# A fused block-sorted attention and PReLU feed-forward kernel: the order of every engine's list read from a fixed table instead of found by a random search

## The chip, the cores and the metric

The kernel runs on one core of a Trainium2 chip. The metric is the device time of one execution in microseconds (us). Five engines work side by side, each through a list of its own in strict order: TensorE (PE, matrix products), VectorE (DVE), ScalarE (ACT), GpSimd (POOL) and SyncE (SP). SP does nothing here but issue DMAs; POOL issues DMAs as well and does copies and memsets between them. A wait at the head of a list holds up everything behind it in that list.

## The reference, cut to what matters

```python
# B, H, S, D = 4, 8, 768, 64; 8 blocks of 96 rows
P = sort_net                      # five rounds: softmax over the rows, then division by the column sums
k_sorted = einsum('bhij,bhjcd->bhicd', P, k_blocks)
v_sorted = einsum('bhij,bhjcd->bhicd', P, v_blocks)
scores = scale * (q_block @ k_sorted_block.T)
attn = exp(scores - max); attn /= attn.sum(-1)
x = (attn @ v_sorted_block)       # -> [3072 tokens, 512]
h = x @ w_in                      # 512 -> 2048
g = max(h, 0) + alpha * min(h, 0)
out = g @ w_out                   # 2048 -> 512
```

## The kernel before, in words

The batch index b runs from 0 to 3. A *group* g = 8 b + i is one block of 96 tokens over all eight heads, so there are 32 groups. For each group the attention makes scores (`s1`, matmul L801 for b = 0 and L798 after that), a row maximum on DVE (`nm` or `nf`, L807), exponentials on ACT, the product with the sorted values (`o`, L854), a reciprocal and a multiplication on DVE (L862, L865). For b = 0 the scores are made again transposed (`s2`, L822 and L813), so the exponentials land as the product needs them. For b > 0 ACT writes `Esb` (eight instructions, L834) and an SP DMA transposes it to `ET` (L839). The result reaches `xT`, token-last, through four PE transposes (L880) and a copy for b < 2, through an SP DMA (L873) after that.

Before a batch can be worked on, its keys and values are mixed with the sorting matrix: `conv_k` (POOL, L701) and `conv_v` (POOL, or ACT or DVE for half of b = 1, L457) spread the loaded rows into `KSz` and `VDz`, then `prep_k` (L714) and `prep_v` (L755) multiply and a copy (L457, ACT or DVE) writes `KT` and `VS`. The queries of b = 0 are turned on PE (`prep_q`); those of b > 0 are loaded by eight DMAs into `QN` (L486) and turned by six SP DMAs into `QTz` (`turn_q`, L494), where turn t holds rows 128 t to 128 t + 127. Group 8 reads turn 0, group 9 turns 0 and 1, group 10 turns 1 and 2.

The feed-forward part is cut into chunks of tokens: groups 0-1, 2-3, then four groups at a time. `ffn1` (L904, four matmuls of 192 or 384 columns) makes one of 16 slices of h for a chunk; ACT makes relu(-h) (L914) and DVE joins the two (L917) into `hT`. `ffn2` (L943) makes a tile of 128 tokens in four parts of four matmuls with 512 columns; a copy (L457) and an SP DMA (L957) store it. The last tile is made in two halves of 256 columns.

All of this is entered by `G.add` as 1226 *operations*, numbered from 0 in the order of the calls, each with its engine (or a choice of ACT and DVE), what it reads and writes, a modelled duration and a priority. `schedule` is a list scheduler: it simulates the engines and always starts, on the engine that can go first, the ready operation of the smallest priority. `search` calls it 2000 times with the priorities shifted at random (500 times for the stage up to the first `xT`, 1500 times for the rest), each promising order being replayed twice with durations up to 8% longer, and keeps the best. `fetched` adds to the PE's simulated time the loading of its program, 256 instructions at a time, `FETCH` = 6200 ns apart at least. After that, `fill` and `idle` put matmuls without use (`warm`, L1070) into gaps that the simulation sees on PE, and `emit` writes each engine's list with the waits that the order needs. Nothing of the simulation runs on the chip: it only fixes the order, the choice of ACT or DVE, and where the warm matmuls stand.

Of the kernel before, what the change touches and what calls it, by code (L numbers as in the profile page):

```python
# [2 lines left out]

# [22 lines left out]
NE = 3  # L26
VSL = 4
EPS = 1e-9
SEARCH = 1500
FIRST = 500  # L30
FETCH = 6200.0
BURST = 140

XLAT = {"pe": 215, "act": 36, "dve": 36, "pool": 80, "sync": 80}
ENGS = ("pool", "sync", "pe", "act", "dve")

# [37 lines left out]
class _Graph:  # L76
# [51 lines left out]
    def fetched(self, op, at, d, f):  # L128

        if f["fills"] and at > 5000:  # L130
            f["n"] += 2 * int(max(at - f["end"], 0) * 0.9 / 215)
        f["fills"] = f["fills"] and op.fills
        n, last = 2 * op.mm, f["n"] + 2 * op.mm
        while f["mark"] < last:
            x = at + d * max(f["mark"] - f["n"], 0) / n
            late = max(f["usable"] - x, 0.0)
            at, x = at + late, x + late
            f["usable"] = x + FETCH
            f["mark"] += 256
        f["n"], f["end"] = last, at + d  # L140
        return at + d

    def ready_at(self, op, e):
        t = 0.0
        for d in op.deps:
            x = self.ops[d]
            if x.eng != e or x.dma:
                lat = XLAT[x.eng]
            else:
# [3 lines left out]
            t = max(t, x.end + lat)  # L153
        return t

    def schedule(self):
        ops = self.ops
        for op in ops:
            op.users, op.eng = [], op.engs
        for op in ops:  # L160
            op.left = len(op.deps)
            for d in op.deps:
                ops[d].users.append(op.idx)
        ready = {e: [] for e in ENGS}

        def release(op):
            op.ready = {}
            for e in op.engs:
                op.ready[e] = self.ready_at(op, e)
                ready[e].append(op)  # L170
# [4 lines left out]
        order = {e: [] for e in ENGS}  # L175
        for op in ops:
            if not op.left:
                release(op)
        done = 0
        while done < len(ops):  # L180
            best = None
            for e in ENGS:
                if not ready[e]:
                    continue
                first = max(free[e], min(o.ready[e] for o in ready[e]))
                op = min((o for o in ready[e] if o.ready[e] <= first + 60), key=lambda o: (o.prio, o.idx))
                first = max(first, op.ready[e])
                if best is None or first < best[0]:
                    best = (first, e, op)
            at, e, op = best  # L190
            for x in op.engs:
                ready[x].remove(op)
            op.eng, op.start = e, at
            free[e], op.end = self.span(op, e, at, free, loads)
            op.pos = len(order[e])
            order[e].append(op)
            done += 1
            for u in op.users:
                ops[u].left -= 1
                if not ops[u].left:  # L200
                    release(ops[u])
        self.order = order
        return max(op.end for op in ops)

    def replay(self, seed):

        rng = random.Random(seed)
        was = [(op.start, op.end) for op in self.ops]
        free = dict.fromkeys(ENGS, 0.0)
        free["pool"] = 400.0  # L210
        loads = [0.0, 0.0, {"n": 2, "mark": 193, "usable": 0.0, "end": 0.0, "fills": True}]
        for op in sorted(self.ops, key=lambda o: (o.start, o.idx)):
            at = max(free[op.eng], self.ready_at(op, op.eng))
            free[op.eng], op.end = self.span(op, op.eng, at, free, loads, 0.08 * rng.random())
        last = max(op.end for op in self.ops)
        self.ends = [op.end for op in self.ops]
        for op, (a, b) in zip(self.ops, was):
            op.start, op.end = a, b
        return last

    def search(self, n, first):

        rng = random.Random(7)
        rank = [op.prio for op in self.ops]
        best = None
        for x in range(FIRST + n):
            if x == FIRST:
                best = None
            lo, hi, part = (-47.5, 3.0, 0.2) if x < FIRST else (0.0, 99.0, 0.1)
            amp = rng.choice((0.1, 0.3, 1.0))  # L230
            for op, p in zip(self.ops, rank):
                op.prio = p + (rng.uniform(-amp, amp) if x % FIRST and lo < p < hi and rng.random() < part else 0.0)
            cost = self.schedule()
            if x < FIRST:
                cost = sum(op.end for op in first)
            if x < FIRST or best is None or cost < best + 1500:
                for seed in (1, 2):
                    late = self.replay(seed)
                    cost += sum(self.ends[op.idx] for op in first) if x < FIRST else late
                cost /= 3  # L240
                if best is None or cost < best:
                    best, rank = cost, [op.prio for op in self.ops]
                    if __import__("os").environ.get("SCHED"):
                        print("search", x, round(cost))
        for op, p in zip(self.ops, rank):
            op.prio = p
        return self.schedule()

    def fill(self, make, unit, first, spans):

# [118 lines left out]
def bass_sinkhorn_attn__then__act_prelu_kernel(  # L369
# [23 lines left out]
    PE, ACT, DVE, POOL, SYNC = ("pe",), ("act",), ("dve",), ("pool",), ("sync",)  # L393
# [3 lines left out]
    bz = sb("bz", [128, 32], BF16)  # L397
# [61 lines left out]
    def t_either(n, mode=1):  # L459
# [4 lines left out]
          w=["P"], prio=-100, dma=(dma_sem("sn"), 0))  # L464
# [266 lines left out]
    first_y, first_x = [], []  # L731
# [233 lines left out]
    def burst(e):  # L965
# [26 lines left out]
    for p in range(2):  # L992
# [14 lines left out]
    for ga, gb in chunks:  # L1007
        w = gb - ga
# [3 lines left out]
        last = gb * BLK // 128  # L1012
# [7 lines left out]
    for g in range(NG + 12):  # L1020
        while fp < len(ffn_plan) and ffn_plan[fp][0] < g:
            pr, kind, a = ffn_plan[fp]
# [7 lines left out]
        b, i = g // NB, g % NB  # L1030
# [84 lines left out]
```

## Time and profile before

| | |
|---|---|
| median of 3 runs | 249.02 us (248.68 to 249.65) |
| the profiled execution, its own time | 249.8 us |
| its span, first to last instruction | 248.1 us |
| PE busy | 234.3 us, 94% |
| DVE, ACT, POOL busy | 171.5, 155.1, 101.1 us (69%, 63%, 41%) |
| warm matmuls (L1070) | 44 |
| mean granted TensorE clock | 0.979 of full speed |

The profile gives, for one execution, the busy time of each engine; the *chain of waits*, followed back from the last instruction, whose pieces stand with their start, length and line; and groups of equal instructions with their count and mean duration. A matmul's duration there is longer than its share of PE's time, since matmuls overlap: four matmuls of 512 columns last 379 ns each, yet take 0.86 us together on the chain. So PE's work is counted from the chain's pieces, not from busy time. A DMA's row gives the time from its issue to its landing.

### The profile page before, as it was taken

What the parts mean: (1) busy time and instruction counts of PE and PEld (TensorE: products, weight loads), DVE (VectorE), ACT (ScalarE), POOL (GpSimd) and SP (SyncE); (2) the same over time, 40 slices, a digit from 0 to 9 for tenths busy, and PEclk for the clock granted to TensorE, in tenths of its full rate; (3) what the DMA queues carried; (4) which work ended last, traced back from release to release, by engine and by line L of the source; (5) the groups of instructions that cost most, each with busy time, mean ns of one, the idle gap of its engine ahead of it and who ended that gap; (6) DMA issues with size and microseconds to landing.
All of it is one profiled execution on the core that took longest, in us unless ns stands there. A gap on an engine that the chain in (4) does not pass through costs nothing.

```text
span 248.1 us, 6269 instructions
## 1 busy us (share of the span) xinstructions
PE 234.3 (94%) x2538; PEld 145.0 (58%) x2538; DVE 171.5 (69%) x347; ACT 155.1 (63%) x423; POOL 101.1 (41%) x146
## 2 busy tenths in 40 slices
PE   6876899999999979999999999999999999999995
PEld 3445567668655636666565666655556555555544
DVE  6764667669787878786679878676869476655510
ACT  5567335596868876786648567965685576455511
POOL 8988902275899967798554103100000000000000
PEclk9999579999999999999999999999999999999999
DMA  6999999999999899989985665532364232301112
GB/s 104 208 211 210 173 215 205 172 196 124 193 85 185 156 170 143 140 121 132 145 135 132 93 159 108 132 94 53 87 122 107 49 103 45 95 11 73 44 45 86
DMA packets 71982, 31.37 MB, mean 126 GB/s; under 512 B 64512, under 2 KB 67344, under 8 KB 71952
## 3 DMA queue, kind: packets, MB, share of 16 engines
q0 software_dynamic: 23408, 13.63, 41.1%
q1 hardware_dynamic: 48544, 17.33, 36.5%
q8 instruction: 20, 0.33, 0.6%
q14 instruction: 10, 0.08, 0.2%
HBM read 27.28 MB, written 6.29 MB: 135 GB/s over the span
## 4 chain that ended last, share of the span: by engine, by line
PE 81%; DMA 8%; ACT 4%; DVE 3%; POOL 2%; issue 2%; POOLq 0%
PE psH L904 31%; PE psYP L943 28%; DMA VST<-in_v_dram 5%; PE psS L943 3%; PE psO L854 3%; PE psS L798 3%; DMA ET<-Esb 3%; PE psYP L755 2%; POOL VDz L457 2%; PE psYP L714 1%; PE psS L813 1%; PE psYP L1070 1%; ACT VDz L457 1%; DVE hT L917 1%; PE psS L822 1%
## 5 line engine op out<-in xcount | busy, mean ns | idle before, releaser
L917 DVE SCALAR_TENSOR_TENSOR hT<-t,omaT,psH 128x384 bf16<-128x384 f32 (+1 forms) x139 | 77.4, 571 | 31.7 <-ACT t L914 29.8
L904 PE MATMUL psH<-xT,w_in_bf 128*128 128x384 bf16 (+1 forms) x556 | 97.8, 312 | 0.6 <-DVE hT L917 0.3
L914 ACT ACTIVATE t<-psH 128x384 f32<-128x384 f32 (+1 forms) x139 | 62.8, 465 | 48.4 <-PE psH L904 44.3
L943 PE MATMUL psYP<-w_out_bf,hT 128*128 128x512 bf16 x336 | 84.7, 379 | 0.3 <-DVE hT L917 0.3
L904 PEld LDWEIGHTS psH<-xT,w_in_bf 128*128 128x128 bf16 x556 | 49.9, 98 | 33.0 <-DVE hT L917 5.9
L834 ACT ACTIVATE Esb<-psS,nf 96x96 bf16<-96x96 f32 x192 | 46.3, 345 | 1.2 <-DVE nf L807 0.9
L943 PEld LDWEIGHTS psYP<-w_out_bf,hT 128*128 128x128 bf16 x336 | 30.4, 98 | 27.4 <-DVE hT L917 0.4
L457 POOL COPY VDz<-VST 64x384 bf16<-64x384 bf16 x40 | 34.0, 851 | 13.6 <-PE psYP L755 11.6
L701 POOL COPY KSz<-KS 64x512 bf16<-64x512 bf16 x36 | 22.2, 618 | 33.0 <-PE psYP L714 21.0
L807 DVE TENSOR_REDUCE nf<-psS 96x8 f32<-96x768 f32 x24 | 22.7, 946 | 0.9 <-PE psS L798 0.9
L865 DVE TENSOR_TENSOR xq<-psO,rec 96x512 bf16<-96x512 f32 x31 | 21.2, 685 | 1.0
L486 POOL DMA_DIRECT2D QN<-in_q_dram x24 | 19.8, 848 | 2.5 <-DMA QTz<-QN 1.2
L854 PEld LDWEIGHTS psO<-VS,ET 112*128 112x128 bf16 x248 | 11.5, 100 | 6.9 <-ACT Esb L834 2.0
L854 PE MATMUL psO<-VS,ET 112*128 112x65 bf16 x248 | 13.1, 196 | 1.8 <-DMA ET<-Esb 1.5
L798 PEld LDWEIGHTS psS<-KT,QTz 128*96 128x96 bf16 x192 | 11.7, 125 | 2.7
L798 PE MATMUL psS<-KT,QTz 128*96 128x96 bf16 x192 | 12.6, 208 | 0.0
L862 DVE RECIPROCAL rec<-psO 96x8 f32<-96x8 f32 x31 | 6.1, 198 | 9.2 <-PE psO L854 9.1
L1070 PE MATMUL psYP<-identb 128*128 128x512 bf16 x34 | 11.3, 468 | 1.0 <-ACT identb L457 1.0
L457 ACT ACTIVATE VS<-psYP 112x512 bf16<-112x512 f32 x13 | 8.9, 687 | 5.0 <-PE psYP L755 3.2
L457 DVE CAST VS<-psYP 112x512 bf16<-112x512 f32 x13 | 9.0, 690 | 3.7 <-PE psYP L755 3.7
L457 ACT ACTIVATE outstg<-psYP 128x512 f32<-128x512 f32 x11 | 6.6, 598 | 7.7 <-PE psYP L943 7.7
L755 PE MATMUL psYP<-BDV,VDz 128*128 128x64 bf16 x192 | 9.5, 193 | 0.5 <-POOL VDz L457 0.5
(139 smaller groups left out, 212.6 us busy)
## 6 DMA issues: line engine op xcount, KB each, us to landing
out_dram<-outstg SPq DMA_DIRECT2D x23, 256.0 KB, 2.3
KS<-in_k_dram POOLq DMA_DIRECT2D x3, 768.0 KB, 31.5
QN<-in_q_dram POOLq DMA_DIRECT2D x24, 96.0 KB, 5.5
w_in_bf<-in_moe_w_in_dram POOLq DMA_DIRECT2D x4, 512.0 KB, 17.3
w_out_bf<-in_moe_w_out_dram POOLq DMA_DIRECT2D x2, 1024.0 KB, 28.6
VST<-in_v_dram POOLq DMA_DIRECT2D x4, 384.0 KB, 31.8
hT<-in_q_dram POOLq DMA_DIRECT2D x1, 768.0 KB, 7.0
VST<-in_v_dram POOLq DMA_DIRECT2D x1, 768.0 KB, 13.4
```

What stands on the lines that cost most here:

```text
L457: return e.activation(o, i, ACTF.Copy) if e is nc.scalar else e.tensor_copy(o, i)
L486: G.add(POOL, lambda e, h=h: e.dma_start(AP(QN, h * 128 + (h // 4) * 64, [[6144, 128], [1024, 6], [1, 64]]), AP(q.tensor, b * HB + h * S * ...
L701: G.add(POOL, lambda e, hp=hp: e.tensor_copy(AP(KSz, hp * 64 * 3072 + u % 3 * 1024 + hp * 64, [[3072, 64], [128, 8], [1, 64]]), AP(KS[n], ...
L798: inst = e.matmul(o, AP(QTz[n], hp * 3072 + h4 * 768 + i * 96, [[6144, 128], [1, 96]]), AP(KT[n], (h4 * 8 + i) * bk, [[ld, 128], [64, 2], ...
L807: G.add(DVE, lambda e: e.tensor_reduce(AP(nx, 0, [[8, 96], [4, 2], [1, 4]]), AP(psX, 0, [[1024, 96], [512, 2], [96, 4], [1, 96]]), AxisLis ...
L834: inst = e.activation(AP(Esb[me], p * 128, [[1024, 96], [64, 2], [1, 48]]), AP(psX, (p // 4) * 512 + (p % 4) * 96, [[1024, 96], [48, 2], [ ...
L854: inst = e.matmul(AP(psZ, hp * 512 + h4 * 68, [[1024, 128], [1, 65]]), AP(ET[me] if far else ET[m], pos(h4, hp) * 96, [[800, nk], [1, 128] ...
L865: G.add(DVE, lambda e: e.tensor_tensor(out=AP(xq[me], 0, [[512, 96], [256, 2], [64, 4], [1, 64]]), in0=AP(psZ, 0, [[1024, 96], [512, 2], [ ...
L904: inst = e.matmul(AP(pt, poff, [[1024, 128], [1, n]]), AP(w_in_bf, kt * DFF + ft * 128, [[KT_TILES * DFF, 128], [1, 128]]), AP(xT, kt * XR ...
L914: G.add(ACT, lambda e: e.activation(AP(t1[tb], 0, [[384, 128], [1, n]]), AP(pt, poff, [[1024, 128], [1, n]]), ACTF.Relu, scale=-1.0), t_ac ...
L917: G.add(DVE, lambda e: e.scalar_tensor_tensor(out=AP(hT, ft * RING + tok % RING, [[FT_TILES * RING, 128], [1, n]]), in0=AP(t1[tb], 0, [[38 ...
L943: inst = e.matmul(AP(bank[0], bank[1], [[1024, 128], [1, n]]), AP(hT, ft * RING + tok % RING, [[FT_TILES * RING, 128], [1, 128]]), AP(w_ou ...
```

## The change

The search and its two helpers (`schedule`, `replay`, `search`) are taken out. A table `SEQ` holds all 1226 operation numbers in one sequence; `arrange` goes through it, puts each operation at the end of its engine's list, and works out the simulated start and end that `fill`, `idle` and `emit` need. A letter behind a number chooses the engine where there is a choice (`d` for DVE, `a` for ACT, none for the first of the two, ACT). Two constants of the simulation change: the distance of program loads becomes 3500, 6150, 7700 or 5200 ns by the time of the load, and the opening burst of 140 tiny matmuls is counted at 9.4 ns each instead of 8.5. The operations themselves, what they compute, their tiles and buffers and the waits' rules stay.

```diff
-import random
-SEARCH = 1500
-FIRST = 500
-FETCH = 6200.0
+SEQ = """
+0 2 10 3 4 11 7 8 1 30 28 9 14 42 43 44 29 45 5 46 47 48 6 49 50 51 147 52 53 54 12 55 56 57 27 58 148 59 60
+61 133 62 63 64 131 65 66 67 132 68 83 69 91 70 84 21 71 89 130 81 72 40 73 87 74 82 75 76 88 77 78 92 79 85
+80 39 93 90 100 94d 95 102 96d 104 103a 16 97 37 86 101d 26 98 107a 108 110d 109d 99a 32 116 106d 111 118
+105a 18 114 38 138 158 117a 115d 149 15 113a 120 150 122 112a 31 347d 151 20 121d 24 23 159 134 312d 13 123d
...
+""".split()
-            f["usable"] = x + FETCH
+            f["usable"] = x + (3500.0 if x < 3000 else 6150.0 if x < 12500 else 7700.0 if x < 30000 else 5200.0)
-    def schedule(self):
...
-    def replay(self, seed):
...
-    def search(self, n, first):
...
+    def arrange(self, table):
+        assert len(table) == len(self.ops)
+        letters = {"p": "pool", "a": "act", "d": "dve"}
         free = dict.fromkeys(ENGS, 0.0)
         free["pool"] = 400.0
         loads = [0.0, 0.0, {"n": 2, "mark": 193, "usable": 0.0, "end": 0.0, "fills": True}]
+        self.order = {e: [] for e in ENGS}
+        done = set()
+        for x in table:
+            op = self.ops[int(x.rstrip("pad"))]
+            e = letters.get(x[-1], op.engs[0])
+            assert e in op.engs and op.deps <= done
+            done.add(op.idx)
+            at = max(free[e], self.ready_at(op, e))
+            op.eng, op.start, op.pos = e, at, len(self.order[e])
             free[e], op.end = self.span(op, e, at, free, loads)
+            self.order[e].append(op)
+        return max(op.end for op in self.ops)
-    G.add(PE, burst, 200 + 8.5 * BURST, r=["bz"], w=["psSw"], prio=-120)
+    G.add(PE, burst, 200 + 9.4 * BURST, r=["bz"], w=["psSw"], prio=-120)
-    total = G.search(SEARCH, first_x)
+    total = G.arrange(SEQ)
```

To read the table one needs a few numbers: 4, 5 and 6 are the loads of q, k and v for b = 0; 147 and 148 the two halves of v for b = 1, 138 its k, 139 to 146 its q; 130 to 133 are `w_in`, 134 and 135 `w_out`; 401 and 402 are v and 403 k for b = 2; 177 to 182 are turns 0 to 5 of the queries of b = 1; 312 and 347 are `conv_v` of b = 1 for two of its eight units; 418 and 434 are the scores of groups 8 and 9. The order of the lists before is the one that the search ends in and that the trace shows. The lists then differ so:

| list | before | with the table |
|---|---|---|
| POOL, loads | q, k, v (b=0), w_in ×4, w_out ×2, k, v, v (b=1), q ×8 (b=1), v, v, k (b=2) | q, k, v (b=0), **v, v (b=1)**, w_in ×4, k (b=1), w_out, q ×2, w_out, **v (b=2)**, q ×6 (b=1), k, v (b=2) |
| SP, turns of b = 1 | 1, 0, 2, 3, 4, 5 | 0, 4, 3, 2, 5, 1 |
| SP, groups 8 to 16 | `ET` of a group, then a turn of b = 2 and the stores, in turns | `ET` of groups 8 to 13 and three stores, then turns of b = 2 one by one between further `ET` |
| POOL, groups 8 on | the eight loads of q (b=2) in one block, then `conv_v` (b=2) | `conv_v` (b=2) and `conv_k` first, loads of q between them |
| `conv_v` of b = 1 on ACT or DVE | 5 on ACT, 3 on DVE | 2 on ACT, 6 on DVE, two of these among the first 54 operations of DVE |
| PE, work in front of the scores of groups 8, 9, 16, 18, 20 (counted from the first `ffn1`) | 28.2, 31.8, 71.4, 83.6, 94.3 us | 27.2, 32.0, 66.1, 74.5, 82.9 us |
| last tile | left half, then right half | right half, then left half |

The last but one row counts the operations in PE's list with the durations that the chain of waits shows for them. All in all 219 of PE's 398 operations stand in another place relative to the rest, and 52 copies change between ACT and DVE.

More of the change, by code (lines that the diff above doesn't have):

```diff
@@ new lines @@
+620 703 751 665a 503 667 621 704 658 646 668 691 659 669 747 705 604d 692 660 629 670 630 631 719a 706 738
+673 739 671 693 674 533 672 740 632 685 633d 675 680 749 681 688 750d 777 686 741 767 689 687 753 846 690
+754a 697 776 768 700 698 778 852 699 701 694 769 702 780 720 682 723 653 779d 707 849 695a 770 802 708 782
+709 724 732 848 721 725 683 742 783a 722 811 729 803 726 696 650 730 813 731 727 733 847 814a 710 728 758
+853 804 743 744 734 781 735 652 759 805 837 812 760 815 755 816a 173 745 736d 764 756 817 757 771 818a 787
@@ new lines @@
+1061 1084 1028 1029 1037 1038 1048 1030 1039 1031 1040 1043 1041 985 1080 1042 1044 1045 1052 1085 1062 1053
+1055 1054 1081 1056 1063 1086 1064 1049 1057 1065 1066 1050d 1069 1067 1087 1115 1068 1070 1082a 1071 1104
+1072 1083 1105 1116 1073 1106 1074 1117 1092 1088 1075 1093 1107 1094 1118 1076 1089 1077 1098 1119a 1095
+1120 1099 1160 1100 1096 1090 1136 1097 1091 1108 1112 1109 1110 1101 1113 1111 1137 1114 1102 1103 1124
+1051 1121 1125 1161 1126 1122 1123 1130 1127 1131 1138 1132 1128 1129 1142 1133 1143 1162 1144 1134 1135
@@ L174, in schedule @@
         loads = [0.0, 0.0, {"n": 2, "mark": 193, "usable": 0.0, "end": 0.0, "fills": True}]
[L175 to L193, printed above, removed]
-            free[e], op.end = self.span(op, e, at, free, loads)
[L195 to L201, printed above, removed]
@@ L202, in schedule @@
-        self.order = order
-        return max(op.end for op in ops)
-    def replay(self, seed):
[L207 to L219, printed above, removed]
@@ L221, in search @@
-    def search(self, n, first):
[L223 to L247, printed above, removed]
```

47 lines of the change are left out of this document (34 added, 13 removed).

## The prediction

> **What bounds the kernel now.** I read the page first, then the chain of waits stretch by stretch, then PE's groups by shape, then the landings of the DMAs.
>
> ```profile
> by line: PE psH L904 41.0%; PE psYP L943 40.0%; PE psS L943 5.9%; PE psS L798 4.4%; PE psO L854 3.5%; PE psYP L714 1.8%; PE psYP L755 1.3%; PE psO L943 1.2%; PE psO L880 0.5%; DVE outstg L457 0.3%; issue 0.0%
> ...
> 229.37 0.86 PE psYP L943 x4
> 230.23 1.30 PE psH L904 x8
> ```
>
> The first row is the chain between 100 and 246 us: its PE shares add up to 99.6%, and PE's pieces stand end to end, as the two below it do. From 100 us on no order can win anything that PE does not do sooner; time won earlier, on the other hand, arrives at the end in full. So the question is what PE wastes before 100 us. These are its groups between the first `ffn1` (30.4 us) and 100 us:
>
> ```profile
> L943 PE MATMUL psYP<-w_out_bf,hT 128*128 128x512 bf16 x67 | 16.9, 379 | 0.3 <-DVE hT L917 0.3
> L904 PE MATMUL psH<-xT,w_in_bf 128*128 128x384 bf16 x80 | 15.6, 327 | 0.4 <-DVE hT L917 0.3
> L904 PE MATMUL psH<-xT,w_in_bf 128*128 128x192 bf16 x108 | 12.8, 255 | 0.2
> L755 PE MATMUL psYP<-BDV,VDz 128*128 128x64 bf16 x128 | 6.4, 193 | 0.5 <-POOL VDz L457 0.5
> L854 PE MATMUL psO<-VS,ET 112*128 112x65 bf16 x80 | 4.3, 197 | 1.8 <-DMA ET<-Esb 1.5 <-ACT ET L845 0.3
> L813 PE MATMUL psS<-identb,nm 96*112 96x96 bf16 x48 | 4.0, 232 | 0.0
> L880 PE MATMUL psO<-identb,xq 96*128 96x96 bf16 x40 | 3.4, 206 | 0.1
> L798 PE MATMUL psS<-KT,QTz 128*96 128x96 bf16 x48 | 3.2, 209 | 0.0
> L1070 PE MATMUL psO<-identb 128*128 128x512 bf16 x10 | 3.0, 379 | 0.0
> L904 PE MATMUL psYP<-xT,w_in_bf 128*128 128x192 bf16 x20 | 2.8, 270 | 0.2 <-ACT KT L457 0.2
> L714 PE MATMUL psYP<-BDM,KSz 128*128 128x64 bf16 x56 | 2.8, 194 | 0.0
> L822 PE MATMUL psS<-QTz,KT 64*112 64x96 bf16 x48 | 2.6, 234 | 0.0
> L1070 PE MATMUL psYP<-identb 128*128 128x512 bf16 x7 | 2.3, 417 | 0.0
> L801 PE MATMUL psS<-KT,QTz 64*96 64x96 bf16 x40 | 1.9, 214 | 0.0
> ```
>
> Their prices when nothing holds them up are pieces of the chain; the two above give 0.215 us for a matmul of 512 columns and 0.1625 us for one of 384:
>
> ```profile
> 36.74 0.34 PE psS L822 x8
> 37.08 0.54 PE psS L813 x8
> ...
> 38.28 0.33 PE psYP L904 x4
> ...
> 38.94 0.31 PE psS L801 x8
> ...
> 94.46 0.37 PE psS L798 x8
> 94.83 0.17 PE psO L880 x4
> ...
> 96.93 0.23 PE psYP L755 x8
> ...
> 100.42 0.24 PE psO L854 x8
> ```
>
> Count by price: L943 67 × 0.215 = 14.4; L904 80 × 0.1625 = 13.0 and 128 × 0.33/4 = 10.6; L755 and L714 (the same shape) 184/8 × 0.23 = 5.3; L854 10 × 0.24 = 2.4; L813 6 × 0.54 = 3.2; L822 6 × 0.34 = 2.0; L801 5 × 0.31 = 1.6; L798 6 × 0.37 = 2.2; L880 10 × 0.17 = 1.7. Together 56.4 us of work in 69.6 us: 13.2 us wasted, in which the 17 warm matmuls (17 × 0.215 = 3.7 us) ran. This is all that there is to win behind the first `ffn1`.
>
> **The change part by part, summed against the profiled execution's own 249.8 us.** That execution lies 0.8 us above the median of the runs shown, 249.02, so the sum's result is moved to the median at the end.
>
> *The start.* The loads run through POOL's queue one after the other.
>
> ```profile
> 2.86 13.41 DMA VST<-in_v_dram
> ...
> L988 POOL DMA_DIRECT2D w_in_bf<-in_moe_w_in_dram x4: 548/563/576, 4.3 to 5.9; - x4
> DMA to landing us min/median/max: 14.4/17.3/20.4
> ...
> L520 POOL DMA_DIRECT2D VST<-in_v_dram x2: 612/618/623, 8.7 to 9.2; - x2
> DMA to landing us min/median/max: 34.8/35.6/36.5
> ...
> 30.43 0.82 PE psH L904 x4
> ```
>
> The v of b = 0 lands at 16.3 us; `w_in` is complete at 5.9 + 20.4 = 26.3, 4.1 us before the first `ffn1`. The two halves of v for b = 1 land at 43.5 and 45.7, 2.2 us apart, so the pair costs 4.4 us of the queue. The table puts the pair ahead of `w_in`, which then lands at 30.7: the cover is gone, and `ffn1` cannot start before 30.7 (+0.3 us). What v of b = 1 gains: it lands at 20.7 instead of 45.7, so `conv_v` can run in the thin stretch before 30 us. But 347 and 312 stand in DVE's list ahead of most copies of `VS` for b = 0 (six of eight are DVE's now). Behind a late v there would wait the copies of `VS`, then `o` of groups 0 and 1, then everything. Between 16.3 us and 347 DVE has three conversions of v, one copy and one row maximum to do, so I have it reach 347 about when that v lands, and the first `ffn1` ready at 30 to 31 us as before. Bounds: 0, and +1.9 us, the length of the one bare stall of the chain in this stretch (next fence, "issue": PE had no work to wait for there, so I read it as a wait for its program). I take +0.3 us, hidden by the next bound.
>
> *From the first `ffn1` to the scores of group 9.* PE's list before holds 31.8 us of work there (128 small `ffn1` matmuls 10.6, eight parts of `ffn2` 6.9, twelve large `ffn1` matmuls 1.95, twelve preparations 2.8, six groups of b = 0 9.6) and takes 71.33 − 30.43 = 40.9 us: 9.1 us of the waste lie here.
>
> ```profile
> 21.76 1.91 issue
> PEclk9999579999999999999999999999999999999999
> ...
> 50.23 0.86 ACT VDz L457
> ...
> 71.33 0.47 PE psS L798 x8
> ...
> L494 SPq DMA_TRANSPOSE QTz<-QN x6: 1312/1860/5588, 51.4 to 65.1; - x6
> DMA to landing us min/median/max: 3.2/5.5/10.0
> ```
>
> Three things make it. Behind the stall the granted clock falls: a slice is a fortieth of the span, 6.2 us, so 0.5 and 0.7 in the fifth and sixth say half clock from about 25 to 34.5 us, and the 4.1 us of it behind 30.4 cost 2.0. ACT's `conv_v` copies (five in this batch at 0.86 us, one of them quoted) stand on the chain between its relu's, while PE waits for `hT`; the table leaves two on ACT. And warm matmuls fill what the old simulation saw as gaps; a new order can only lessen the need for them (in gaps they cost nothing; if all 17 stood in the way, 3.7 us). Worth up to 7 us, then, but a DMA caps it. The scores of group 9 need turns 0 and 1. Before, the last turn landed at 65.1 + 3.2 = 68.3 us. With the table turn 1 is the last of the six; the turns start when the q's have landed, which is 2.2 us later than 51.4 because half of v for b = 2 goes first; in exchange that much less load runs beside the turns, so I keep 68.3 for the last. The scores of group 9 can come forward from 71.33 to 68.3 at most: 3.0 us. PE would need 30.7 + 32.0 = 62.7 us without any waste, so it may still waste 5.6 us of the 9.1 and reach the cap. I take 2.0 us. Bounds: 3.0, and −1.9 if the stall and half clock come once more.
>
> *From the scores of group 9 to 100 us.* Here 13.2 − 9.1 = 4.1 us are wasted.
>
> ```profile
> 80.01 0.84 POOL VDz L457
> ...
> 85.99 6.39 DMA ET<-Esb
> ...
> ET<-Esb SPq DMA_TRANSPOSE x24, 3.0
> ```
>
> PE ran out of work behind two chains: POOL's copies for b = 2, the last of five in a row at 0.84 us, held back by the block of eight loads of q in front of them; and the transpose of group 10, 6.39 us from issue to landing where the median of all 24 is 3.0. It flew together with turns of b = 2 and loads. The table takes both out of the way: `conv_v` stands before the loads of q, and the `ET` of groups 8 to 13 go ahead of all turns of b = 2. What is late next: `prep_k` of b = 2 and its turns, needed only for group 16. Its scores, though, are asked for 5.3 us of PE work earlier than before. I take 2.0 us. Bounds: 3.5, and −1.5, the idle time that PE had once for an `ET` (in the row of L854 above), should it come again for a turn of b = 2.
>
> *Behind 100 us, and the end.* PE is full, and the scores stand 5 to 11 us of PE work earlier than before for groups 16 to 20, so the `ET` have more cover: nothing to win, and a list in which ACT or DVE is late is covered by what the longer lead leaves. The halves of the last tile change places and each ends with a copy and a store: 0.
>
> Sum: 249.8 − 2.0 − 2.0 = 245.8 us; at the level of the median, 245.0 us.
>
> By the Trainium skill, "TensorE: Matmul & The Clock Gate", Part 1 on the clock gate, the clock falls to half only behind a whole idle window of about 3.4 us. The trace does not agree: the clock fell behind a stall of 1.9 us. By the page a table with gaps under 3.4 us wins the 2.0 us of half clock for certain; by the row it can lose them to the next stall of 1.9 us, and the sum goes by the row.
>
> **The rivals.**
>
> *All of it comes back.* PE reaches the cap (3.0) and the stretch behind it loses almost nothing (3.5): 249.02 − 6.5 = 242.5 us. For it: five separate causes of waste are moved at once. Against it: a list in strict order meets its waits one by one, and the simulation's durations are not the chip's.
>
> *A wait takes the place of the one removed.* PE comes to the scores of group 8 and 9 earlier and stands before turn 1; the `ET` still collide, now with the loads of k and v for b = 2, which are issued later than before. The turns end 2.2 us later, at 70.5, the gain up to group 9 shrinks to 71.3 − 70.5 = 0.8 us, and behind it nothing comes back: 249.02 − 0.8 = 248.2 us. For it: the first turn starts 2.2 us later, and one that was needed first has become the last.
>
> *Slower: the start slips.* The place is DVE's list in front of the copies of `VS`, the price a later first `ffn1`. If v of b = 1 lands later than 20.7 us, or PE's program stall of 1.9 us falls behind it, the first `ffn1` moves to 32.6 us, half clock reaches 2 to 4 us further into it (1 to 2 us more lost, say 1.5), and only half of the 2.0 behind group 9 comes back: 249.02 + 1.9 + 1.5 − 1.0 = 251.4 us. It decides from the point where the start's slip exceeds what is won up to group 9, 2.0 us. For it: the cover of `w_in` falls from 4.1 to 0 us. Against it: v of b = 0 landed exactly when the queue's order says.
>
> **How the numbers follow.** The forecast 0.45, all of it 0.20, the wait in place 0.13, slower 0.22. The forecast's own range is 243.5 to 246.8 us, 0.75 more or 0.9 less in each of the two stretches. For eight in ten I reach down to 241.5, 1 us under the best case, and up to 250.8, into the slower case; the worst bounds of both stretches together (249.02 + 1.9 + 1.5 = 252.4) stay outside. Faster by over 0.5% (what a measurement of this kernel can tell from no change, 1.25 us) means under 247.8: the first two and a little of the third, 0.66. Within it 0.12, slower 0.22.
>
> **What would show it.** Right: the clock row without the dip or with a shorter one; the first `ffn1` at about 30.7; the scores of group 9 at 68 to 70 us, waiting for nothing or for a turn; no ACT `VDz` copies on the chain around 50 us; `ET` of group 10 landing in under 5 us; the wasted PE time between 30.4 and 100 us down from 13.2 to about 9 us. Wrong: PE waiting for `w_in` or DVE before the first `ffn1`, a second dip of the clock, a bare stall behind 30 us, or scores of groups 16 to 20 that wait for turns of b = 2.

## The result, and the profile after

| | before | with the table |
|---|---|---|
| median of 6 runs | 249.07 us (247.56 to 250.40) | 246.02 us (245.37 to 247.29) |
| ratio, 95% interval | | 0.9865 (0.9832 to 0.9898) |
| the profiled execution, its own time | 249.8 us | 245.37 us |
| its span | 248.1 us | 243.4 us |
| matmuls without use, `warm` | 44 | 28 |
| half clock | 24.2 to 34.5 us | 19.6 to 36.7 us |

The table makes the kernel 1.35% faster; the forecast was 245.0 us. Ratios here and below leave out executions in a slower state, medians do not, which lifts most that of "before, copies on DVE" (250.35 us without them). The sum behind the forecast had three terms, and all three came out otherwise: the start slipped, and more than forecast was won behind it.

The chain of waits of the kernel after (start, length, engine, tile, line; L429 is the copy helper, L732 `prep_v` of b = 0, L876 `ffn1`, L770 the scores of b > 0):

```profile
20.88 0.56 DVE VDz L429
21.45 0.69 DVE VS L429
22.15 0.86 DVE nm L779
...
23.02 2.19 DVE VDz L429
...
25.23 1.32 DVE VS L429 x2
...
26.59 0.64 PE psYP L732 x16
...
33.34 1.39 PE psH L876 x8
...
69.89 0.49 PE psS L770 x8
```

The first `ffn1` starts at 33.34 us where it was 30.43: a slip of 2.9 us. The two `VDz` rows are 347 and 312, the early `conv_v` copies in DVE's list; copies of `VS` stand behind them, and PE's next `prep_v` behind those. The scores of group 9 start at 69.89 us, 1.44 us earlier than before, in spite of the slip.

The clock row of the page after, beside the one of before in the prediction:

```profile
PEclk9996559999999999999999999999999999999999
```

The dip begins earlier and lasts 17.1 us instead of 10.2; behind the first `ffn1`, though, 3.4 us of it are left, where it was 4.0.

PE's groups of weight loads between the first `ffn1` and 100 us, in the kernel after (each matmul has one; they are counted here because some matmul records are missing):

```profile
L876 PEld LDWEIGHTS psH<-xT,w_in_bf 128*128 128x128 bf16 x192 | 16.2, 100 | 6.3 <-DVE hT L889 1.4
L915 PEld LDWEIGHTS psYP<-w_out_bf,hT 128*128 128x128 bf16 x80 | 7.1, 98 | 6.2 <-ACT outstg L429 0.4
L727 PEld LDWEIGHTS psYP<-BDV,VDz 128*128 128x128 bf16 x128 | 5.3, 98 | 1.5 <-DVE VS L429 0.2
L826 PEld LDWEIGHTS psO<-VS,ET 112*128 112x128 bf16 x88 | 3.8, 98 | 0.9
L770 PEld LDWEIGHTS psS<-KT,QTz 128*96 128x96 bf16 x58 | 3.4, 125 | 0.6 <-ACT Esb L806 0.4
L686 PEld LDWEIGHTS psYP<-BDM,KSz 128*128 128x128 bf16 x80 | 3.4, 98 | 0.9
L785 PEld LDWEIGHTS psS<-identb,nm 96*112 96x112 bf16 x48 | 3.3, 142 | 0.4
L852 PEld LDWEIGHTS psO<-identb,xq 96*128 96x128 bf16 x40 | 2.5, 98 | 0.9 <-DVE xq L837 0.3
L794 PEld LDWEIGHTS psS<-QTz,KT 64*112 64x112 bf16 x48 | 1.9, 138 | 1.0 <-issue 0.5 <-DVE nm L779 0.4
L876 PEld LDWEIGHTS psYP<-xT,w_in_bf 128*128 128x128 bf16 x20 | 1.8, 108 | 0.0
L773 PEld LDWEIGHTS psS<-KT,QTz 64*96 64x96 bf16 x40 | 1.3, 120 | 1.6 <-ACT ET L817 1.1 <-ACT t L886 0.4
```

With the prediction's prices, in us: L915 80 × 0.215 = 17.2; L876 212, of which 128 are small, 10.6, and 84 large, 13.7; L727 and L686 26 × 0.23 = 6.0; L826 2.6; L785 3.2; L794 2.0; L773 1.6; L770 2.7; L852 1.7. That is 61.3 us of work in the 66.7 us from 33.3 on: 5.4 us wasted, where it was 13.2. By the last but one row of the table of lists 32.0 us of it stand in front of the scores of group 9, which came 69.89 − 33.34 = 36.55 us behind the first `ffn1`: 4.5 us of waste there (9.1 before) and 0.9 us behind (4.1 before).

The `ET` transposes of groups 8 to 17, issue on SP and time to landing:

```profile
L811 SPq DMA_TRANSPOSE ET<-Esb x10: 1213/1219/1425, 69.8 to 113.5; - x10
...
DMA to landing us min/median/max: 2.8/4.4/5.5
```

None takes 6.39 us any more, and PE waits for none. (The 6.39 us one of before is the fourth `ET`, so group 11's and not group 10's, as the prediction has it.) Behind 100 us the chain is PE (94% by this line, 99.6% before) with scraps of others:

```profile
by line: PE psH L876 39.6%; PE psYP L915 37.7%; PE psS L915 6.0%; PE psS L770 3.8%; PE psO L826 3.1%; PE psYP L686 1.4%; DVE hT L889 1.2%; PE psO L915 1.2%; PE psYP L727 1.0%; issue 0.8%; ACT t L886 0.7%; DVE VS L429 0.5%; ACT VS L429 0.5%;
```

### The profile page after: what moved, and what is told of

It reads as the page before. It is cut to its first block, busy times and chain, and to the rows that moved or that the text cites. A ratio compares the mean times of both kernels' runs of the same rounds, so it can differ in the third digit from the quotient of the medians.

```text
span 243.4 us, 6215 instructions
## 1 busy us (share of the span) xinstructions
PE 229.2 (94%) x2494; PEld 144.6 (59%) x2522; DVE 175.5 (72%) x349; ACT 154.3 (63%) x421; POOL 100.0 (41%) x146
## 4 chain that ended last, share of the span: by engine, by line
PE 82%; DVE 6%; DMA 5%; POOL 3%; issue 1%; ACT 1%; POOLq 0%
PE psH L876 32%; PE psYP L915 29%; DMA VST<-in_v_dram 5%; PE psS L915 4%; PE psS L770 3%; PE psO L826 3%; PE psYP L727 2%; PE psYP L686 2%; DVE hT L889 2%; PE psS L785 1%; DVE VS L429 1%; DVE VDz L429 1%; PE psS L794 1%; PE psS L773 1%; DVE xq L837 1%
## 5 line engine op out<-in xcount | busy, mean ns | idle before, releaser
L876 PE MATMUL psH<-xT,w_in_bf 128*128 128x384 bf16 (+1 forms) x556 | 99.0, 312 | 0.3
L915 PE MATMUL psYP<-w_out_bf,hT 128*128 128x512 bf16 x309 | 78.3, 379 | 1.4
L876 PEld LDWEIGHTS psH<-xT,w_in_bf 128*128 128x128 bf16 x556 | 49.9, 98 | 30.5 <-DVE hT L889 4.3
L915 PEld LDWEIGHTS psYP<-w_out_bf,hT 128*128 128x128 bf16 x336 | 31.3, 98 | 29.7 <-ACT outstg L429 0.4
L429 POOL COPY VDz<-VST 64x384 bf16<-64x384 bf16 x40 | 34.2, 856 | 16.3 <-PE psYP L727 14.3
L429 ACT ACTIVATE VS<-psYP 112x512 bf16<-112x512 f32 x18 | 12.5, 694 | 3.0 <-PE psYP L727 2.7
L826 PEld LDWEIGHTS psO<-VS,ET 112*128 112x128 bf16 x248 | 11.3, 99 | 3.8
L826 PE MATMUL psO<-VS,ET 112*128 112x65 bf16 x248 | 12.9, 196 | 0.0
L770 PEld LDWEIGHTS psS<-KT,QTz 128*96 128x96 bf16 x192 | 11.4, 125 | 2.4 <-ACT Esb L806 0.6
L770 PE MATMUL psS<-KT,QTz 128*96 128x96 bf16 x192 | 12.6, 209 | 0.0
L429 ACT ACTIVATE KT<-psYP 128x512 bf16<-128x512 f32 x12 | 7.1, 595 | 3.9 <-PE psYP L686 3.0
L727 PE MATMUL psYP<-BDV,VDz 128*128 128x64 bf16 x192 | 9.6, 193 | 0.1
L915 PE MATMUL psS<-w_out_bf,hT 128*128 128x512 bf16 (+1 forms) x47 | 9.4, 343 | 0.1
L1042 PE MATMUL psYP<-identb 128*128 128x512 bf16 x26 | 9.0, 470 | 0.5 <-ACT identb L429 0.5
```

Of the source, the lines that this page charges most:

```text
L429: return e.activation(o, i, ACTF.Copy) if e is nc.scalar else e.tensor_copy(o, i)
L770: inst = e.matmul(o, AP(QTz[n], hp * 3072 + h4 * 768 + i * 96, [[6144, 128], [1, 96]]), AP(KT[n], (h4 * 8 + i) * bk, [[ld, 128], [64, 2], ...
L826: inst = e.matmul(AP(psZ, hp * 512 + h4 * 68, [[1024, 128], [1, 65]]), AP(ET[me] if far else ET[m], pos(h4, hp) * 96, [[800, nk], [1, 128] ...
L876: inst = e.matmul(AP(pt, poff, [[1024, 128], [1, n]]), AP(w_in_bf, kt * DFF + ft * 128, [[KT_TILES * DFF, 128], [1, 128]]), AP(xT, kt * XR ...
L915: inst = e.matmul(AP(bank[0], bank[1], [[1024, 128], [1, n]]), AP(hT, ft * RING + tok % RING, [[FT_TILES * RING, 128], [1, 128]]), AP(w_ou ...
```

## The experiments

All are the kernel after with a few numbers of the table moved, unless the name begins with "before". In the diffs `seq` is the table `SEQ`, handed to `arrange`, and `move(seq, words, after)` takes operations out of the table and puts them in behind another one. Where copies or loads come later than in the table, `idle` adds no matmuls behind 52 us, so that new gaps of the simulation bring none. Time is the median; the kernel before, run beside each group of kernels, had 249.5 us (first four of the table), 249.8 (next four), 250.5 (the rest), so across groups the ratios are to be compared; where an expectation gives a time, the ratio times 249.5 is to be compared with it, as that was about the level when it was set. The last three columns are from the one profiled execution of each: the start of the first `ffn1` matmul and of the scores of group 9 in us, and how long the clock was at half. In the kernel after they are 33.3, 69.8 and 17.1.

| kernel | time | ratio to before, 95% | first `ffn1` | scores g9 | half clock before 60 us |
|---|---|---|---|---|---|
| conv_v on ACT | 243.03 | 0.9778 (0.9728 to 0.9829) | 30.3 | 67.6 | 17.1 us |
| memset away | 245.18 | 0.9872 (0.9811 to 0.9932) | 32.1 | 69.5 | 20.5 |
| DMA order as before | 249.45 | 1.0022 (0.9981 to 1.0062) | 33.3 | 70.8 | 20.5 |
| late ACT copies | 246.57 | 0.9904 (0.9879 to 0.9929) | 30.0 | 71.1 | 10.2 |
| fed start | 242.25 | 0.9727 (0.9672 to 0.9783) | 30.9 | 66.3 | none |
| load block alone | 249.69 | 0.9973 (0.9937 to 1.0008) | 33.1 | 70.6 | 20.5 |
| before, no warm | 250.16 | 1.0035 (1.0001 to 1.0070) | 30.1 | 72.6 | 17.1 |
| before, copies on DVE | 251.43 | 1.0022 (0.9979 to 1.0066) | 29.5 | 71.6 | 3.4 |
| fed less | 242.69 | 0.9688 (0.9624 to 0.9752) | 30.0 | 66.0 | none |
| w_in first | 243.14 | 0.9710 (0.9637 to 0.9783) | 29.1 | 68.3 | none |
| late v | 243.43 | 0.9725 (0.9665 to 0.9785) | 30.0 | 67.5 | 13.7 |
| all loads in order | 244.19 | 0.9754 (0.9694 to 0.9815) | 29.1 | 68.7 | 3.4 |

### The start: DVE's list, or something else?

Two copies change their engine, from DVE to ACT:

```diff
+    seq = [{"347d": "347a", "312d": "312a"}.get(w, w) for w in seq]
-    total = G.arrange(SEQ)
+    total = G.arrange(seq)
```

> The two early conv_v copies (312 and 347) go from DVE to ACT, at the same place of the table; nothing else moves. Theory that DVE's list sets the start: the copies of VS come 2.2 to 2.75 us earlier (312 took 2.19 us, 347 0.56 us), PE's prep_v of unit 5 starts near 24 instead of 26.59 us, the first ffn1 near 30.7 instead of 33.3 us, and the time falls by that much, from 246.0 to 243 to 243.7 us. ACT has idle time for both (2.16 us ahead of the exponentials of group 0, two copies of 0.86 us). Rival that PE's program load or w_in (landed at 30.0 us) sets the start: prep_v of unit 5 not before 25.5 us or the first ffn1 not before 32.5 us, time 245.5 to 246.5 us.

Measured 243.03 us. Its chain of waits:

```profile
22.34 1.22 DVE VS L429 x2
...
23.61 0.64 PE psYP L732 x16
...
30.37 1.39 PE psH L876 x8
```

Both late copies of `VS` are done 3.0 us earlier, `prep_v` of unit 5 starts at 23.61 instead of 26.59, the first `ffn1` 3.0 us earlier. At the scores of group 9 2.2 us of it are left, as in the span (241.2 us): the half clock reaches 4.5 us past the first `ffn1` instead of 3.4, which at half speed is worth some 0.6 us of the difference. So the slip was the place of two copies in DVE's list; undoing it is worth 0.9% of the kernel and beats both kernels.

Why did 312 take 2.19 us, when its like takes 0.56? In the kernel after POOL had a memset beside it (POOL's timeline: start, length):

```profile
22.70 0.89 POOL L965 DMA_DIRECT2D w_out_bf<-in_moe_w_out_dram  x1
23.58 1.40 POOL L510 MEMSET KSz<- 128x1536 f32 x1
24.90 1.67 POOL L458 DMA_DIRECT2D QN<-in_q_dram  x2
```

```diff
+    seq = move(seq, "13", "135")
```

> 312 stays on DVE in front of the copies of VS, but POOL's memset of KSz (1.40 us, at 23.58 us, inside the 2.19 us of 312) is moved behind the second load of w_out, so that only DMA issues of POOL stand beside 312. Theory that the two engines' accesses to SBUF get in each other's way, and the memset is what holds 312: 312 takes 0.55 to 0.9 us, the first ffn1 comes at about 32 us, time 244.4 to 245 us. Rival that 312 waits for something else (its data, or POOL's DMA issues beside it): it still takes over 1.5 us, first ffn1 at 33.0 to 33.6 us, time 245.5 to 246.5 us.

The two timelines of that kernel, DVE's 312 and what POOL did then:

```profile
22.95 1.13 DVE L429 COPY VDz<-VST 64x384 bf16<-64x384 bf16 x1
```

```profile
22.15 0.89 POOL L965 DMA_DIRECT2D w_out_bf<-in_moe_w_out_dram  x1
23.04 1.66 POOL L458 DMA_DIRECT2D QN<-in_q_dram  x2
```

312 falls from 2.19 to 1.13 us, more than the 0.55 to 0.9 expected: the memset held it for about 1.1 us, and beside DMA issues it still takes twice the 0.56 of 347. The first `ffn1` comes 1.2 us earlier, as expected; the time does not follow (ratio 0.9872 against 0.9865). In the profiled execution the half clock reached 5.3 us past the first `ffn1` instead of 3.4, worth 1 us, and 0.3 us of the gain were left at the scores of group 9. The other executions of the two kernels do not bear this out (their mean clocks, 0.957 to 0.965, are alike in both), and the interval is wide enough to hide 1.2 us: why nothing was gained stays open. By the Trainium skill, "SBUF — State Buffer", section "SBUF: two separate sides", DVE (in some of its modes) and GpSimd contend for one pair of ports, which the one that starts first holds for its whole instruction, while the other waits. The trace agrees in part: in the kernel after, the copy ended at 25.21, 0.23 us behind the memset's end, but it had started 0.56 us before the memset, when POOL was at a DMA issue; what held it until then no run shows.

### The clock

In the traces the granted clock changes only at ends of stretches of 3.41 us (10.24 us of half clock before and 17.07 after are three and five of them). These are such stretches (length, PE busy, granted clock), of the kernel before, then of the kernel after:

```profile
20.81:24.22 3.41, 1.50 (x62) 1.00 1.08 217
24.22:27.64 3.42, 3.23 (x59) 0.50 1.06 148
```

```profile
16.22:19.63 3.41, 1.91 (x65) 1.00 1.05 216
19.63:23.04 3.41, 3.03 (x53) 0.50 1.05 209
33.28:36.69 3.41, 3.41 (x33) 0.50 1.15 174
```

A stretch in which PE was busy for 44% or 56% ends in half clock, and the second has no idle piece over 1.04 us in it; the clock comes back behind a full one. So PE was given work without use in its gaps (f32, of which three matmuls of 256 columns last 1.49 us, so that few instructions are added). `feeds` holds the operation in front of which, the number, the columns and the place of each:

```diff
+    feeds, lst = {116: (3, 256, -1), 114: (2, 128, -1), 120: (1, 256, -1), 151: (2, 128, -1), 124: (3, 128, -1), 156: (1, 256, 512), 165: (1, 256, 512), 195: (3, 256, 512)}, []
+    for op in G.order["pe"]:
+        if op.idx in feeds:
+            n, cols, off = feeds[op.idx]
...
+            lst.append(x)
+        lst.append(op)
```

> As the run with 312 and 347 early on ACT (243.0 us), and 16 more matmuls without use (f32, 128 or 256 columns) in PE's gaps between 15 and 30 us. In all six profiles so far the granted clock fell at the end of a stretch of 3.41 us in which PE was busy for 44 to 67% of it, and stretches of 70% or more never did it. Theory that a fed PE keeps the full clock: no half clock between 14 and 35 us, the first ffn1 at 29.5 to 30.4 us (w_in lands at 30.0), and 2 to 3 us less time, 240 to 241.2 us. Rival that the added matmuls stand in PE's way or bring its program load forward: the clock falls all the same or PE stalls for 1 us or more before 28 us, first ffn1 after 31 us, time 243 to 245.5 us.

The first two stretches, fed, and the chain in front of the first `ffn1`:

```profile
14.16:17.57 3.41, 2.24 (x37) 1.00 1.02 207
17.57:20.99 3.42, 3.42 (x92) 1.00 1.04 211
```

```profile
29.55 1.49 PE psH L1052 x6
31.04 0.66 PE psH L876 x8
```

The half clock is gone (mean 0.999). The ratio goes from 0.9778 to 0.9727 (the intervals overlap), and the span from 241.2 to 239.9 us: 1.3 us, half of what was expected. The added matmuls in front of the first `ffn1` ended at 31.04 us, 1.2 us behind the landing of `w_in` (29.80). So those were left out:

```diff
-    feeds = {..., 165: (1, 256, 512), 195: (3, 256, 512)}
+    feeds = {..., 165: (1, 256, 512)}
```

> The fed start without its last piece: the six passes of matmuls without use right in front of the first ffn1 lasted 1.49 us there and ended at 31.04 us, 1.0 us behind the landing of w_in (about 30.0 us). Theory that they held the first ffn1 and that the clock stays up without them: first ffn1 at 30.0 to 30.4 us at full clock, 0.7 to 1.0 us faster than the fed start, 241.2 to 241.6 us. Rival that the gap which they filled makes the clock fall: half clock for 3.4 us or more behind 28 us, 242.5 to 243.5 us.

First `ffn1` at 30.0 us at full clock, as expected, but the scores of group 9 gain only 0.3 of the 0.9 us, and the median, 242.69 us, is not below that of the fed start (the ratio is, by 0.4%, within the two intervals). What PE waits for between 37 and 100 us in this kernel (us in total, times, longest), and its chain:

```profile
PE psYP L915 <- DMA w_out_bf<-in_moe_w_out_dram: 0.4, 1, 0.4
PE psS L770 <- DMA QTz<-QN: 0.2, 1, 0.2
```

```profile
62.67 3.21 DMA QTz<-QN
66.01 0.53 PE psS L770 x8
```

Now the load of `w_out` and turn 1, the last of the six, come last: the cap that the prediction set on the gain binds here, where PE is 3.8 us earlier at this point than with the table alone. It costs PE 0.2 us, and the load of `w_out` 0.4.

That feeding removes the half clock is shown. That a low busy share brings it is not the whole rule, and the expectation above (44 to 67%) had not looked past the start of the kernels. One stretch of the kernel with `w_in` first (below), in which PE waited for `w_out`:

```profile
37.77:41.19 3.42, 1.36 (x12) 1.00 1.57 173
```

It was 40% full and the clock stayed up behind it, as it did behind one of 57% in the kernel before (89.1 to 92.5 us) and behind ones of 53 and 55% in two others, while one of 36% (79.8 to 83.2 us, in the first kernel of the next section) brought half clock. What else decides stays open.

### The second stretch: block of loads, or transposes in each other's way?

```diff
+    seq = move(seq, "412 416 413 411 417 415 410 414", "572")
+    seq = move(seq, "427", "437")
+    seq = move(seq, "443", "467")
+    seq = move(seq, "473 503", "497")
+    seq = move(seq, "533", "553")
```

> The table, with the DMAs of the queries of b = 2 put back where the kernel before has them: the eight loads of q in one block of POOL's list ahead of six of its conv_v copies for b = 2, and the turns of b = 2 between the ET of groups 9 to 14. Theory that this order made the waste between the scores of group 9 and 100 us (3.2 us less of it with the table): 1.5 to 3.5 us slower than with the table, 247.5 to 249.5 us, with POOL's VDz copies on the chain of waits and an ET of 5 us or more from issue to landing near 80 us. Rival that PE's own order, which leaves more ffn work ready, saved it: at most 0.7 us slower, under 246.8 us.

Measured 249.45 us: all that the table had won is gone. `ET` and who waited for one, in this kernel:

```profile
  PE psO L826: 1.6, 1
...
DMA to landing us min/median/max: 2.8/4.7/8.8
```

To part the two, the first line of that diff alone, the block of loads:

> The table with the eight loads of q for b = 2 in one block of POOL's list, but the turns of b = 2 where the table has them, behind ET of groups 8 to 13. With both put back it was 249.5 us, 3.8 us of it lost between the scores of groups 11 and 12 and 1.5 us behind those of group 15. Theory that POOL's copies behind the block cost the 3.8 us, and the ET that fly with the turns the rest: 3 to 4 us slower than with the table, 248.6 to 249.6 us less the 1.5 us, so 248.0 to 249.0 us, loss between the scores of groups 11 and 12 as there, ET of group 14 under 5 us. Rival that the ET beside the turns cost nearly all: 246 to 247 us.

Measured 249.69 us, and by the ratio 248.8, inside the expected range. Its chain:

```profile
81.00 0.82 POOL VDz L429
...
81.88 0.82 POOL VDz L429
...
82.75 0.41 PE psYP L727 x8
83.16 1.24 PE psH L876 x4
```

POOL's copies behind the block hold PE's `prep_v` of b = 2 as before; the scores of group 12 start at 88.4 us, 4.3 us later than with the table (0.8 of it at the scores of group 9 already), and behind PE's idle time half clock comes once more (83.1 to 86.5 us; four `ffn1` matmuls take 1.24 instead of 0.65 us). By the ratios the block alone takes back 1.1 of the 1.35%, and with the turns it is 0.5% more, 1.2 us, about what PE waited for the `ET` in the first kernel's profile; but the two intervals overlap. So the larger part of the second term was POOL's list; what the `ET` cost is not resolved. Nor need an `ET` fly with a turn to be slow: in the second kernel one took 6.8 us, with the first turn of b = 2 issued only at 102.2 us, and PE waited for none.

### The first stretch: which part saved 4.5 us?

The prediction had named ACT's copies, the warm matmuls, and the start. Copies late on ACT again:

```diff
+    seq = move(seq, "312a", "282")
+    seq = move(seq, "347a", "288")
+    seq = [{"355d": "355a", "390d": "390a"}.get(w, w) for w in seq]
```

> Five conv_v copies of b = 1 go to ACT as in the kernel before, four of them late: 312 and 347 behind ACT's relu pieces of groups 2 and 3 (near 50 us), 355 and 390 where the table has them. To be compared with the run in which 312 and 347 are early on ACT. Theory that late ACT copies of 0.86 us hold PE's hT: the first ffn1 at 30.7 us as there, then 1 to 2.6 us lost between 45 and 66 us, 244.5 to 246 us, with ACT VDz on the chain of waits. Rival that they lie beside other work: within 0.5 us of that run, 243 to 244 us.

Measured 246.57 us, 3.5 more than with 312 and 347 early on ACT and more than the 1 to 2.6 expected. (Six of the eight copies are on ACT here, the table's own two among them; the kernel before had five.) Up to the scores of group 7 no more than 0.4 us is lost; then 355 and 390 stand on the chain, in front of a relu and between the exponentials and a `prep_v`:

```profile
59.87 0.86 ACT VDz L429
...
69.14 0.85 ACT VDz L429
```

Does the reverse help the kernel before?

```diff
+    for n in (312, 347, 351, 355, 390):
+        op = G.ops[n]
+        G.order["act"].remove(op)
+        op.eng = "dve"
+        G.order["dve"].append(op)
+    G.order["dve"].sort(key=lambda op: op.start)
```

> The kernel before with its five conv_v copies of ACT (312, 347, 351, 355, 390) entered in DVE's list at the times they had; all else in its order. Theory that the copies hold ACT's relu pieces, and so PE's hT: the three copies of 0.86 us leave the chain of waits near 50 us and 1.3 to 2.6 us are won, 246.5 to 248 us. Rival that DVE's pieces then wait as ACT's did, or that another wait stands right behind: within 0.7 us, 248.5 to 250 us.

No: ratio 1.0022. The place on the chain is taken by DVE, whose maximum, copy and join follow each other:

```profile
52.32 0.86 DVE nm L807
...
53.21 0.69 DVE VDz L457
53.91 0.43 DVE hT L917
```

The kernel before without its warm matmuls behind the first `ffn1`:

```diff
-    G.fill(warm, 215, ident_op, [(5000, first_y[0].start), (ffn_ops[0].start + 1, ffn_ops[1].start)])
-    G.idle(warm, 215, {"psY": (psYP, 0), ("psP", 0): (psYP, 512), ("psH", 0): (psH, 0), ("psH", 1): (psH, 512),
-                       "psO0": (psO, 0), "psO1": (psO, 512)}, ffn_ops[0].start, 130e3, 450)
+    G.fill(warm, 215, ident_op, [(5000, first_y[0].start)])
```

> The kernel before without its 17 matmuls without use behind the first ffn1. Theory that they lie in gaps: 248.5 to 250 us, no change beyond 0.7 us. Rival that they stand in the way, as the prediction bounds it: 1.5 to 3.7 us faster, 245.5 to 248 us. Rival that they keep the clock up: a further fall of the granted clock behind 36 us, slower by 1.5 us or more.

250.16 us, no gain, though the half clock lasted until 41.8 instead of 34.5 us: they were not in the way. Last, the early v, in the kernel with 312 and 347 out of DVE's early list:

```diff
+    seq = move(seq, "147 148", "135")
+    seq = move(seq, "351a", "282")
+    seq = move(seq, "312d", "288")
+    seq = move(seq, "347d 310a", "314")
+    seq = move(seq, "346 309 311", "350")
```

> The run with the start mended (312 and 347 off DVE's early list, 243.0 us), but v of b = 1 loaded behind w_out, as late as in the kernel before (landing near 45 us), and the first conv_v copies of b = 1 moved behind that: 312, 347 and 310 on DVE and 351 on ACT near 50 us, 346, 309, 311 on POOL near 50 us. Theory that the early v is what saved PE time up to the scores of group 9, since it takes half of the copies out of the stretch of 46 to 70 us: 1.3 to 3 us lost between the scores of groups 6 and 9, 244.3 to 246 us. Rival that PE's order alone saved it: within 0.5 us, 242.6 to 243.5 us.

243.43 us: the scores of group 9 come at 67.5 us as with the early v. None of the three parts alone brings the 4.5 us; in the new order late copies on ACT cost 3.5 us, but at another place. Where they were saved can be counted with the same prices: up to the scores of group 7 the kernel before has 18.6 us of work in 25.8 us, the kernel after 17.5 in 21.0, so 3.7 of the 4.5 us are won there, the stretch in which the chain before runs through ACT and DVE from 48.68 to 54.62 us and the chain after for 0.82 us (`ET`, 49.13). Which moves of the order, PE's among them, won them was not tried one by one and stays open.

### When PE is early enough, do the loads bind?

The run that was fed less, with `w_in` in front of v for b = 1 again:

```diff
+    seq = move(seq, "147 148", "130")
+    seq = move(seq, "346 309", "144")
+    seq = move(seq, "312a", "282")
+    seq = move(seq, "347a", "288")
```

> The same with the loads of w_in put back in front of the two halves of v for b = 1, and the conv_v copies that would wait for that v moved back: 346 and 309 on POOL behind two loads of q, 312 and 347 on ACT to about 50 us, where they had done no harm. Theory that w_in is what the first ffn1 waits for once the clock stays up: w_in lands near 26 us, first ffn1 at 28.8 to 29.6 us, 0.5 to 1.3 us faster than the run with v first, 240.0 to 240.9 us. Rival that the early v pays: the first ffn1 comes as early, but 0.5 to 2 us are lost between the scores of groups 5 and 9, 241.2 to 242.5 us.

And the late v, fed less, with two more moves:

```diff
+    seq = move(seq, "178", "177")
+    seq = move(seq, "401", "145")
```

> The late v run (243.4 us) with the fed start (without its last piece), turn 1 of the queries second instead of last, and the half of v for b = 2 that goes ahead of six of the q's for b = 1 put behind them. Theory that nothing but the start, half clock and the loads' order held these runs: w_in lands near 26 us, first ffn1 at 28.8 to 29.6 us at full clock (30.5 at half clock in the late v run), the scores of group 9 without a wait for a turn at 64.5 to 65.5 us (67.5 there), 241.0 to 241.9 us. Rival that the next wait (PE's work is then ahead of the conv_v copies of b = 1, landing near 45 us) takes the gain: over 1 us lost between the scores of groups 6 and 9, 242.3 to 243.5 us.

Both start `ffn1` at 29.1 us, as expected, and both give it back, as the rivals said: by the ratios 242.3 and 243.4 us, 0.5 and 1.6 us above the run that was fed less. The chain of the second:

```profile
27.37 19.68 DMA VST<-in_v_dram
...
50.77 0.84 POOL VDz L429
...
53.00 0.41 PE psYP L686 x8
```

v lands at 47.05 us, POOL's four copies and two of k come behind it, and PE loses 4.4 us beyond its work between the scores of groups 7 and 8, where the kernel with the late v and a later start lost 1.0; 3.4 us of half clock lie in it. So a late v binds once PE is early. That the early v pays is less sure: fed less with the table's own loads has the lowest ratio, 0.9688, but `w_in` first (0.9710), the late v (0.9725) and the fed start (0.9727) lie within its interval.

## Why the prediction came out right

The number, 246.0 us for 245.0, is in part luck. The forecast for the first stretch came out near because two errors in it cancelled, and one of the prediction's own signs of being wrong, PE waiting for DVE in front of the first `ffn1`, is what happened.

*The start* (+0.3 us forecast) failed: +2.9. The step was that DVE would reach 347 "about when that v lands", at no cost. It did: v landed at 20.2 and 347 started at 20.88. What was left out is the second copy, 312, in front of four copies of `VS`, and that it would take 2.19 us beside a memset. The prediction's landing of `w_in` was computed rightly (30.7 forecast, 30.0 seen) but it was not what came last. The rival "the start slips" had the place right, DVE's list in front of the copies of `VS`, and 32.6 us for the first `ffn1`; its reasons, a late v or a stall for PE's program, were not the ones, and it lost because it expected little behind.

*Up to group 9* (−2.0 at the scores of group 9) came out at −1.44, as the sum of larger numbers: 2.9 us of slip, 0.2 us of work more and 4.5 us of waste less, where the prediction had expected some 2.3. The cap at 68.3 us did not bind: turn 1 landed at 67.0, 2.9 us ahead of the scores. It binds once the start is mended and PE fed. Of the causes named, half clock grew as a whole and hardly changed behind the first `ffn1` (3.4 us for 4.0), and ACT's copies and the warm matmuls alone are not it.

*Behind group 9* (−2.0, bounds to 3.5) was −3.2. The mechanism, POOL's block of loads, was right and is shown for most of it; the size was near the bound, because PE lost 3.2 of its 4.1 us of waste there and not half. The part put down to colliding `ET` is not shown.

*Half clock* was taken as set by one bare stall. No such stall is needed: it came behind stretches of 3.41 us that were 56 and 58% full with no idle piece over 1.04 and 0.63 us, and it stayed away when the gaps were fed. Behind some stretches as empty it did not come, so the rule is not known in full.

The terms give 2.9 + 0.2 − 4.5 − 3.2 = −4.6 us; the two profiled executions differ by 4.4, and the ratio says 3.4. The profiled one of the table is its fastest, 0.65 us below the median, and that of the kernel before lies 0.7 us above its median, so the traces flatter the table by about 1 us.

## What to carry to other kernels

A table made under a model is as good as the durations in it: two small copies of DVE, one of which took 2.19 us beside POOL where the other took 0.56, made the start slip by 2.9 us, nearly the 3.4 us that were won in all. Look for the first operation that everything else waits for, and read which list holds it; sending two copies to an engine that was idle was worth two thirds of what the whole table had brought. When a start is mended, look at once for the next cap; here it was the loads.

## What was not expected of the hardware

- PE's clock fell to half without an idle stretch of 3.41 us. In the traces (the end of the programs left out) it fell behind twelve stretches of that length in which PE was busy for 36 to 58% of the time and two of 67 and 68%, with no idle piece over 2.18 us in any of them; it stayed up behind four of 40, 53, 55 and 57% and behind seven between 60 and 67%. It came back behind full stretches (twice behind 93 and 96%), though not behind each: six of 99 to 100% left it at half. The Trainium skill, "TensorE: Matmul & The Clock Gate", Part 1, has it fall after an idle window of about 3.4 us (and tells of one kernel in which short idle pieces between groups of matmuls made it swing, with no length for them): the length of the window agrees, the need for it to be idle does not.
- A copy on DVE from SBUF to SBUF (64 x 384) took 0.51 us in the kernel before with POOL at rest, 0.56 beside two short memsets of 0.31 and 0.53 us, 1.13 beside POOL's DMA issues, 1.17 beside POOL's own copies and 2.19 beside the memset of `KSz`, while the copies of `VS` (from PSUM) took 0.67 to 0.70 us beside DMA issues and beside that memset.
